# A state-space scan beside sliding-window attention: the last states of each group kept in another column order

## The chip, the cores and the metric

The kernel runs on one core of one Trainium2 chip. The metric is the device time of one execution in microseconds (us). PE is the matrix engine, DVE the vector engine, ACT the scalar engine, POOL and SP the two others; each executes its own stream of instructions in order, and semaphores connect them.

## The reference

Two independent parts, each on an input of 2048 positions by 448 channels, give the two halves of the output's last axis.

```python
# part A: a diagonal complex state-space model, 448 states
Lam_bar = exp(dt * Lam);  B_bar = ((Lam_bar - 1) / Lam)[:, None] * Bmat
h = 0
for t in range(2048):
    h = Lam_bar * h + B_bar @ x[t]
    y[t] = 2 * Re(Cmat @ h) + x[t] * Dskip
# part B: attention of 16 heads of 28, each query sees 8 keys, 2 positions apart
q, k, v = split(x @ wqkv)
attn = softmax(q . k[pos - 2*w] / sqrt(28), over w = 0..7, masked where pos - 2*w < 0)
out = (sum_w attn[w] * v[pos - 2*w]) @ wo
```

## The kernel before

**Part A** treats a complex state as two real rows: 64 states fill 128 partitions (64 real, 64 imaginary parts), so there are 7 blocks `m`. A multiplication by a power of Lam_bar is a 128x128 matrix, built for the powers 1, 2, 3, 4, 8, 12, 16, 32, ... up to 1024 (`mats`). Positions are cut into 512 groups of 4; `b` is the place in a group, and a column of 512 stands for the group. 512 groups are again 128 chunks `c` of 4 groups `a`, in column order `(c a)`.

- `level1` computes for each b and m the state within the group (`h[b]`, 512 columns): four matmuls with x, and one from the b before; ACT evicts it from PSUM (L450). `h[3]` is each group's own last state.
- `scan` gives the state at the end of each chunk of 16 positions. Its head (L460, L463) adds up the four groups of a chunk: the moving operands are the columns of one `a`, so every fourth column. Seven doubling steps (L470) then add the sum shifted by 1, 2, ... 64 chunks; the shifted operand lies in `pbuf`, with 64 zero columns ahead of it. After each step ACT copies the sum to `pbuf` (L474), and after the last to every fourth column of `G` (L476).
- `ends` gives the true state at the end of the three other groups of each chunk, from `h[3]` and from the carry, which is the chunk sum one chunk earlier, read from `G` at every fourth column. Six matmuls per m (L489, 1152 moving columns in all), and an eviction of 384 elements to every fourth column of `G` (L490). `G` starts with a zero column, so that `G[:, m, 0:512]` is the state ahead of each group.
- `correct` adds the carry to `h[0]` to `h[2]` (L496 to L498), and `y` forms the output of 128 groups for one b from seven blocks and the skip term (L509, L512, L515), 16 tiles in all.

The seven blocks are worked in two halves, m 0 to 3 and m 4 to 6 (`MH`). The program's order is level1, scan of half 0, level1, scan of half 1, ends 0, the corrections of half 0, ends 1, then y for b = 3, and per b the corrections of half 1 and y.

**Part B** projects q, k, v on PE, and forms the products with shifted keys and values on DVE (`qk`, L159 to L161; `pv`, L215 and L220), partly summed on PE (L164). `pv` goes through four groups of four positions; each group's result is transposed on PE (`pt_o`, L241, and for the last group L238, which also sums the last parts), evicted, multiplied by `wo` (L248) and stored. The products of a key group alternate between two `pr` buffers.

**Order.** The program emits part B's `pv` ahead of part A's level1; the framework decides at build time how each engine's stream interleaves them, after data dependences and the program's order as priority. PSUM tiles of the tag `mm` have three buffers, which level1, scan, ends, corrections and y share.

Of the kernel before, what the change touches and what calls it, by code (L numbers as in the profile page):

```python
# [12 lines left out]
f32 = mybir.dt.float32  # L13
bf16 = mybir.dt.bfloat16
# [4 lines left out]
NCH = 128  # L19
# [3 lines left out]
NF = 512  # L23
# [8 lines left out]
NM = 7  # L32
PL = 64
NST = 7
PAD = 64
MH = ((0, 4), (4, 7))
# [217 lines left out]
class PartA:  # L254
# [170 lines left out]
    def alloc_h(self):  # L425
        pool = self.pool
        self.h = [pool.tile([NCH, NM, 4 * NCH], bf16, name="h0", tag="xT1"),
                  pool.tile([NCH, NM, 4 * NCH], bf16, name="h1", tag="xT0"), pool.tile([NCH, NM, 4 * NCH], bf16, name="h2", tag="q1"),
                  pool.tile([NCH, NM, 4 * NCH], bf16, name="h3")]
        self.pbuf = [[pool.tile([NCH, m1 - m0, PAD + NCH], bf16, name=f"pbuf{m0}{i}") for i in range(2)]  # L430
                     for m0, m1 in MH]
        for pb in self.pbuf:
            for t_ in pb:
                self.nc.gpsimd.memset(t_[:, :, 0:PAD], 0.0)
        self.G = pool.tile([NCH, NM, 1 + NF], bf16, name="G", tag="q0")
        self.nc.gpsimd.memset(self.G[:, :, 0:1], 0.0)

    def level1(self, mh):
        nc, cx = self.nc, self.cx
        for b in range(4):  # L440
            for m in range(*MH[mh]):
                ps = cx.ps([NCH, 4 * NCH], f32, "l1", "mm")
                for k in range(KT):
                    nc.tensor.matmul(ps[:], lhsT=self.Bcat[:, k, m, :],  # L444
                                     rhs=self.xT[:, b, k, :],
                                     start=(k == 0), stop=(b == 0 and k == KT - 1))
                if b:
                    nc.tensor.matmul(ps[:], lhsT=self.mats[1][:, m, :], rhs=self.h[b - 1][:, m, :],  # L448
                                     start=False, stop=True)
                nc.scalar.copy(self.h[b][:, m, :], ps[:])  # L450

    def scan(self, mh):
        nc, cx = self.nc, self.cx
        M, v = self.mats, self.h[3]
        m0, m1 = MH[mh]
        pb = self.pbuf[mh]
        ps = cx.ps([NCH, m1 - m0, NCH], f32, "l2", "mm")
        for m in range(m0, m1):
            vm = v[:, m, :].rearrange("p (c a) -> p a c", a=4)
            nc.tensor.matmul(ps[:, m - m0, :], lhsT=cx.ident[:], rhs=vm[:, 3], start=(m == m0), stop=False,  # L460
                             skip_group_check=True)
            for i, p_ in enumerate((4, 8, 12)):
                nc.tensor.matmul(ps[:, m - m0, :], lhsT=M[p_][:, m, :], rhs=vm[:, 2 - i], start=False,  # L463
                                 stop=(i == 2), skip_group_check=True)
        nc.scalar.copy(pb[0][:, :, PAD:], ps[:])
        for s_ in range(NST):
            shf = 1 << s_
            src, dst = pb[s_ % 2], pb[(s_ + 1) % 2]
            for m in range(m0, m1):
                nc.tensor.matmul(ps[:, m - m0, :], lhsT=M[T << s_][:, m, :],  # L470
                                 rhs=src[:, m - m0, PAD - shf:PAD - shf + NCH], start=False, stop=True,
                                 skip_group_check=True)
            if s_ < NST - 1:
                nc.scalar.copy(dst[:, :, PAD:], ps[:])  # L474
            else:
                nc.scalar.copy(self.G[:, m0:m1, 1:].rearrange("p m (c a) -> p m c a", a=4)[:, :, :, 3], ps[:])  # L476

    def ends(self, mh):
        nc, cx = self.nc, self.cx
        M, v = self.mats, self.h[3]  # L480
        for m in range(*MH[mh]):
            vm = v[:, m, :].rearrange("p (c a) -> p a c", a=4)
            hp = self.G[:, m, 0:NF].rearrange("p (c a) -> p a c", a=4)[:, 0]
            ps = cx.ps([NCH, 3, NCH], f32, "gt", "mm")
            mm = [(cx.ident[:], vm[:, 0:3], 0, 3), (M[4][:, m, :], vm[:, 0:2], 1, 3), (M[8][:, m, :], vm[:, 0], 2, 3),
                  (M[4][:, m, :], hp, 0, 1), (M[8][:, m, :], hp, 1, 2), (M[12][:, m, :], hp, 2, 3)]
            for i, (l_, r_, c0, c1) in enumerate(mm):
                o_ = ps[:, c0:c1] if c1 - c0 > 1 else ps[:, c0]
                nc.tensor.matmul(o_, lhsT=l_, rhs=r_, start=(i == 0), stop=(i == 5), skip_group_check=True)  # L489
            nc.scalar.copy(self.G[:, m, 1:].rearrange("p (c a) -> p a c", a=4)[:, 0:3], ps[:])  # L490

    def correct(self, b, mh):
        nc, cx = self.nc, self.cx
# [131 lines left out]
```

## Time and profile before

| | |
|---|---|
| median of three runs | 171.19 us (170.5 to 171.29) |
| the profiled execution: time, span | 171.67 us, 169.9 us |
| granted PE clock | 0.997 |
| PE busy | 158.5 us (93%) |
| DVE busy | 146.0 us (86%) |
| ACT busy | 108.6 us (64%) |
| POOL busy | 3.6 us (2%) |
| DMA | 14.22 MB, mean 84 GB/s |

The span runs from the first to the last instruction; the time holds what lies around it as well. Busy shares are means over stages with different limits. In the groups, a number behind a line is the duration of one instruction, in ns; for a matmul that is its latency, and matmuls that follow each other overlap. Part A's level1 lies between 58 and 101 us, scans and ends between 81 and 120 us, and the y tiles from 121 us to the end.

### The profile page before, as it was taken

How to read it: one execution, taken by the hardware profiler on the slowest of the kernel's cores; microseconds unless marked ns; L12 is line 12 of the kernel's file. 1: busy time of each engine (PE TensorE's matmuls, PEld its weight loads, DVE VectorE, ACT ScalarE, POOL GpSimd, SP SyncE). 2: the span in 40 equal slices, each digit the busy share in tenths (PEclk: the TensorE clock that was granted, in tenths of full speed). 3: DMA queues.
4: the chain of work that ended last, by engine and by line, in shares of the span. 5: the costliest groups of instructions: out<-in, count | busy, mean ns of one | idle time of the engine just before them, and what ended most of it. 6: DMA issues, size and time to landing. Idle time of an engine off the chain costs nothing.

```text
span 169.9 us, 2983 instructions
## 1 busy us (share of the span) xinstructions
PE 158.5 (93%) x1152; PEld 92.1 (54%) x1162; DVE 146.0 (86%) x186; ACT 108.6 (64%) x206; POOL 3.6 (2%) x30
## 2 busy tenths in 40 slices
PE   7786999989999999999999999889999999999992
PEld 4453565555646564545664566436555655557750
DVE  1279999999999999999979999999999999990330
ACT  3194376647995788645568467999845765475241
POOL 8000000000000000000000000000000000000000
PEclk9999999999999999999999999999999999999998
DMA  5999756279945150000000000000122131212131
GB/s 167 298 287 196 117 105 161 85 207 203 165 88 152 62 161 4 0 0 0 0 4 0 0 0 4 0 0 0 54 86 82 46 120 58 81 54 100 41 106 54
DMA packets 23829, 14.22 MB, mean 84 GB/s; under 512 B 15855, under 2 KB 22923, under 8 KB 23815
## 3 DMA queue, kind: packets, MB, share of 16 engines
q1 hardware_dynamic: 23744, 14.03, 31.8%
q8 instruction: 9, 0.15, 0.4%
q14 instruction: 5, 0.04, 0.1%
q10 hardware_dynamic: 71, 0.01, 0.0%
HBM read 5.05 MB, written 3.67 MB: 51 GB/s over the span
## 4 chain that ended last, share of the span: by engine, by line
PE 63%; ACT 16%; DVE 13%; DMA 3%; issue 2%; ACTq 1%
PE l L444 12%; PE y_ps L512 12%; PE qkv_ps L141 8%; PE wo_ps L248 8%; DVE mat L395 4%; PE lg L164 4%; ACT Bcat L82 3%; PE l L448 3%; DMA drow<-in_A_Dskip_dram 3%; PE gt L489 2%; DVE pr L159 2%; ACT pbuf L474 2%; PE co L496 2%; PE pt_o L238 2%; DVE q L90 2%
## 5 line engine op out<-in xcount | busy, mean ns | idle before, releaser
L141 PE MATMUL qkv_ps<-wqkv_nat,xbT 112*128 112x448 bf16 x192 | 40.1, 352 | 1.9 <-DVE xbT L88 1.2
L215 DVE TENSOR_TENSOR pvb<-attn,vd 128x1792 bf16<-128x1792 bf16 (+1 forms) x33 | 34.0, 1050 | 0.0
L159 DVE TENSOR_TENSOR pr<-q,kd 128x3584 bf16<-128x3584 bf16 x16 | 31.7, 2018 | 1.2 <-PE lg L164 1.1
L444 PE MATMUL l<-xaT,Bcat 128*128 128x512 bf16 x106 | 29.1, 379 | 0.3
L141 PEld LDWEIGHTS <-xbT 112*128 112x128 bf16 x192 | 17.8, 97 | 16.9 <-DVE xbT L88 1.5
L220 DVE TENSOR_TENSOR pvb<-pvb 128x1792 bf16<-128x1792 bf16 x25 | 26.9, 1075 | 0.0
L450 ACT CAST h<-l 128x512 bf16<-128x512 f32 x28 | 16.3, 595 | 7.4 <-PE l L448 6.6
L512 PE MATMUL y_ps<-Ccat,h 128*128 128x448 bf16 x84 | 18.8, 352 | 0.0
L160 DVE TENSOR_TENSOR pr<-pr 128x1792 bf16<-128x1792 bf16 x16 | 16.8, 1083 | 0.0
L515 ACT CAST ya<-y_ps 128x448 bf16<-128x448 f32 x16 | 8.5, 534 | 12.4 <-PE y_ps L512 9.6
L444 PEld LDWEIGHTS <-Bcat 128*128 128x128 bf16 x112 | 10.6, 98 | 10.2 <-issue 0.2
L395 DVE TENSOR_TENSOR mat<-Dm,Scat 128x896 bf16<-128x896 f32 x13 | 14.1, 1082 | 0.0
L248 PE MATMUL wo_ps<-wo_p,oT 112*128 112x448 bf16 x64 | 13.5, 354 | 0.4
L498 ACT CAST h<-co 128x512 bf16<-128x512 f32 x21 | 11.3, 623 | 0.0
L82 ACT CAST yb<-wo_ps 128x448 bf16<-128x448 f32 x14 | 7.6, 541 | 4.9 <-PE wo_ps L248 4.7
L82 ACT CAST vd<-qkv_ps 128x448 bf16<-128x448 f32 x16 | 8.3, 534 | 3.3 <-PE qkv_ps L141 3.0
L82 ACT COPY xbT<-pt_x 112x512 bf16<-112x512 bf16 x12 | 7.0, 582 | 5.0 <-PE pt_x L134 5.0
L82 ACT CAST kd<-qkv_ps 128x448 bf16<-128x448 f32 x12 | 6.4, 532 | 5.6 <-PE qkv_ps L141 5.6
L512 PEld LDWEIGHTS <-h 128*128 128x128 bf16 x84 | 7.2, 98 | 4.8
L248 PEld LDWEIGHTS <-oT 112*128 112x128 bf16 x64 | 5.6, 98 | 7.4 <-ACT oT L82 3.0
L164 PE MATMUL lg<-pr,ident 128*128 128x128 bf16 x112 | 8.9, 219 | 0.4 <-DVE pr L161 0.4
L161 DVE TENSOR_TENSOR pr<-pr 128x896 bf16<-128x896 bf16 x16 | 9.2, 613 | 0.0
(131 smaller groups left out, 219.2 us busy)
## 6 DMA issues: line engine op xcount, KB each, us to landing
out_dram<-yb SPq DMA_DIRECT2D x16, 112.0 KB, 1.7
out_dram<-ya SPq DMA_DIRECT2D x16, 112.0 KB, 1.7
xb_sb<-in_B_x_dram SPq DMA_DIRECT2D x3, 448.0 KB
wqkv_nat<-in_B_wqkv_dram SPq DMA_DIRECT2D x3, 392.0 KB, 6.8
kd<-kd SPq DMA_DIRECT2D x1, 784.0 KB, 5.4
vd<-vd SPq DMA_DIRECT2D x1, 784.0 KB
kd<-kd SPq DMA_DIRECT2D x1, 588.0 KB, 4.2
vd<-vd SPq DMA_DIRECT2D x1, 588.0 KB
```

Of the source, the lines that this page charges most:

```text
L82: nc.scalar.copy(out, in_)
L141: nc.tensor.matmul(ps[:], lhsT=self.xT[j // 4][:, k, j % 4, :], rhs=self.wn[:, k, which, :], start=(k == 0), stop=(k == KT - 1))
L159: V.tensor_tensor(pr[:].rearrange("p d j h -> p j d h"), self.q[hf][:], self.kd[:, off:off + HJ], op=ALU.mult)
L160: V.tensor_tensor(pr[:, 0:14], pr[:, 0:14], pr[:, 14:28], op=ALU.add)
L164: nc.tensor.matmul(lgs[w // 4][:, w % 4, :], lhsT=cx.ident[:], rhs=pr[:, d].rearrange("p j h -> p (j h)"), start=(d == 0 and w % 4 == 0), ...
L215: V.tensor_tensor(t_[:, c0:c1], at[:, w, jl0 + c0:jl0 + c1, :].unsqueeze(2).to_broadcast([NCH, c1 - c0, DH, H]), self.vd[:, off + c0:off + ...
L220: V.tensor_tensor(acc[:, 0:n], acc[:, 0:n], t_[:, 0:n], op=ALU.add)
L248: nc.tensor.matmul(ps[:], lhsT=oT[:, kt, :], rhs=self.wo_p[:, kt, :], start=(kt == 0), stop=(kt == KT - 1))
L395: eng.tensor_tensor(t_[:], self.Dm[:].unsqueeze(1).unsqueeze(1).to_broadcast([NCH, NM, 2, PL]), scal.unsqueeze(3).to_broadcast([NCH, NM, 2 ...
L444: nc.tensor.matmul(ps[:], lhsT=self.Bcat[:, k, m, :], rhs=self.xT[:, b, k, :], start=(k == 0), stop=(b == 0 and k == KT - 1))
L450: nc.scalar.copy(self.h[b][:, m, :], ps[:])
L512: nc.tensor.matmul(ps[:], lhsT=self.state(m, r, b), rhs=self.C[:, m, :], start=False, stop=(m == NM - 1), skip_group_check=True)
```

## The change

The 512 columns of `h[3]` are stored as `(a c)` instead of `(c a)`: all chunks of the first group of a chunk, then those of the second, and so on. The order is made when ACT evicts `h[3]` (PSUM is then read with a step of four columns). The scan's head and the ends then take contiguous moving operands. The scan's last step is evicted to `pbuf` as the others are, and `ends` reads the carry from there, one column back. A seventh matmul per m copies the chunk sums into the ends' PSUM tile, and one eviction of 512 elements brings the tile back to `(c a)` in `G`: PSUM is read with a step of 128 columns, and `G` is written contiguously from its second column on. `G` is one column wider per m.

```diff
-        self.G = pool.tile([NCH, NM, 1 + NF], bf16, name="G", tag="q0")
+        self.G = pool.tile([NCH, NM, 2 + NF], bf16, name="G", tag="q0")
 ...
     def level1(self, mh):
-                nc.scalar.copy(self.h[b][:, m, :], ps[:])
+                if b < 3:
+                    nc.scalar.copy(self.h[b][:, m, :], ps[:])
+                else:
+                    nc.scalar.copy(self.h[b][:, m, :].rearrange("p (a c) -> p a c", a=4),
+                                   ps[:].rearrange("p (c a) -> p a c", a=4))
     def scan(self, mh):
-            vm = v[:, m, :].rearrange("p (c a) -> p a c", a=4)
+            vm = v[:, m, :].rearrange("p (a c) -> p a c", a=4)
 ...
-            if s_ < NST - 1:
-                nc.scalar.copy(dst[:, :, PAD:], ps[:])
-            else:
-                nc.scalar.copy(self.G[:, m0:m1, 1:].rearrange("p m (c a) -> p m c a", a=4)[:, :, :, 3], ps[:])
+            nc.scalar.copy(dst[:, :, PAD:], ps[:])
     def ends(self, mh):
+        hc = self.pbuf[mh][NST % 2]
         for m in range(*MH[mh]):
-            vm = v[:, m, :].rearrange("p (c a) -> p a c", a=4)
-            hp = self.G[:, m, 0:NF].rearrange("p (c a) -> p a c", a=4)[:, 0]
-            ps = cx.ps([NCH, 3, NCH], f32, "gt", "mm")
-            mm = [(cx.ident[:], vm[:, 0:3], 0, 3), (M[4][:, m, :], vm[:, 0:2], 1, 3), (M[8][:, m, :], vm[:, 0], 2, 3),
-                  (M[4][:, m, :], hp, 0, 1), (M[8][:, m, :], hp, 1, 2), (M[12][:, m, :], hp, 2, 3)]
+            vm = v[:, m, :]
+            hp = hc[:, m - MH[mh][0], PAD - 1:PAD - 1 + NCH]
+            ps = cx.ps([NCH, NF], f32, "gt", "mm")
+            mm = [(cx.ident[:], vm[:, 0:3 * NCH], 0, 3), (M[4][:, m, :], vm[:, 0:2 * NCH], 1, 3),
+                  (M[8][:, m, :], vm[:, 0:NCH], 2, 3), (M[4][:, m, :], hp, 0, 1), (M[8][:, m, :], hp, 1, 2),
+                  (M[12][:, m, :], hp, 2, 3), (cx.ident[:], hc[:, m - MH[mh][0], PAD:PAD + NCH], 3, 4)]
 ...
-            nc.scalar.copy(self.G[:, m, 1:].rearrange("p (c a) -> p a c", a=4)[:, 0:3], ps[:])
+            nc.scalar.copy(self.G[:, m, 1:1 + NF].rearrange("p (c a) -> p c a", a=4),
+                           ps[:].rearrange("p (a c) -> p c a", a=4))
```

More of the change, by code (lines that the diff above doesn't have):

```diff
@@ L480, in ends @@
         M, v = self.mats, self.h[3]
+        hc = self.pbuf[mh][NST % 2]
         for m in range(*MH[mh]):
-            vm = v[:, m, :].rearrange("p (c a) -> p a c", a=4)
-            hp = self.G[:, m, 0:NF].rearrange("p (c a) -> p a c", a=4)[:, 0]
-            ps = cx.ps([NCH, 3, NCH], f32, "gt", "mm")
-            mm = [(cx.ident[:], vm[:, 0:3], 0, 3), (M[4][:, m, :], vm[:, 0:2], 1, 3), (M[8][:, m, :], vm[:, 0], 2, 3),
-                  (M[4][:, m, :], hp, 0, 1), (M[8][:, m, :], hp, 1, 2), (M[12][:, m, :], hp, 2, 3)]
+            vm = v[:, m, :]
[4 more added lines that the diff above has]
+                  (M[12][:, m, :], hp, 2, 3), (cx.ident[:], hc[:, m - MH[mh][0], PAD:PAD + NCH], 3, 4)]
             for i, (l_, r_, c0, c1) in enumerate(mm):
-                o_ = ps[:, c0:c1] if c1 - c0 > 1 else ps[:, c0]
-                nc.tensor.matmul(o_, lhsT=l_, rhs=r_, start=(i == 0), stop=(i == 5), skip_group_check=True)
-            nc.scalar.copy(self.G[:, m, 1:].rearrange("p (c a) -> p a c", a=4)[:, 0:3], ps[:])
+                nc.tensor.matmul(ps[:, c0 * NCH:c1 * NCH], lhsT=l_, rhs=r_, start=(i == 0), stop=(i == 6),
+                                 skip_group_check=True)
+            nc.scalar.copy(self.G[:, m, 1:1 + NF].rearrange("p (c a) -> p c a", a=4),
+                           ps[:].rearrange("p (a c) -> p c a", a=4))
     def correct(self, b, mh):
```

## The prediction

> **What bounds the kernel now.** I read the page first, then the vector engine's waits, the chain of waits, the table of stretches, and the groups by shape. The page's bars say that two engines take turns as the limit:
>
> ```profile
> PE   7786999989999999999999999889999999999992
> DVE  1279999999999999999979999999999999990330
> ACT  3194376647995788645568467999845765475241
> ```
>
> From about 30 us to 153 us VectorE (DVE) is full; TensorE (PE) is full from the start of part A to the end; ScalarE (ACT) is full for a few slices around 105 us. The table of stretches (columns: length, then busy time of PE, weight loads, DVE, ACT) puts numbers on the three phases that matter:
>
> ```profile
> 103.40:112.20 8.80, 7.78 (x51) 4.41 (x50) 8.80 (x11) 8.68 (x15) 0.00 (x0) 1.00 0.01 2
> 127.10:142.10 15.00, 14.78 (x105) 8.37 (x105) 15.00 (x16) 9.53 (x19) 0.00 (x0) 1.00 0.23 78
> 153.30:169.90 16.60, 13.46 (x127) 8.66 (x125) 2.63 (x4) 5.78 (x11) 0.00 (x0) 0.97 0.21 70
> ```
>
> In the first ACT has no free moment, while PE idles 1.0 us. Later PE and DVE are both full. After DVE's last product, at 153.3, PE still has work to the end: not because DVE was late but because PE is behind it. The chain of waits shows that (start, length, what):
>
> ```profile
> 115.53 2.13 PE gt L489 x12
> 117.66 0.45 PE pt_o L241 x8
> ...
> 155.86 1.79 PE pt_o L238 x32
> ```
>
> The four groups of part B's accumulator leave DVE at 112.1, 127.1, 142.1 and 153.3 (starts and lengths in DVE's timeline); PE takes up their first transposes at 117.5, 132.3, 146.6 and 155.7 (its timeline). So PE runs 5.4, 5.2, 4.4 and 2.4 us behind. **PE's order from 115 us on is the path, and whatever makes PE arrive earlier shortens the kernel until it meets DVE.**
>
> The vector engine's own waits hold one line of interest:
>
> ```profile
> DVE pr L159 <- PE lg L164: 1.1, 1, 1.1
> ```
>
> At 86.96 DVE waits for PE, which has just come through the first scan's head.
>
> **The strided operands, priced.** The groups by shape:
>
> ```profile
> L470 PE MATMUL l<-pbuf,mat 128*128 128x128 bf16 x49 | 5.1, 220 | 0.2
> L463 PE MATMUL l<-h,mat 128*128 128x128 bf16 x21 | 3.4, 295 | 0.0
> L490 ACT CAST G<-gt 128x384 bf16<-128x384 f32 x7 | 7.3, 1040 | 0.9 <-PE gt L489 0.9
> L476 ACT CAST G<-l 128x512 bf16<-128x512 f32 x1 | 1.3, 1314 | 0.0
> L474 ACT CAST pbuf<-l 128x512 bf16<-128x512 f32 x6 | 3.5, 588 | 1.5 <-PE l L470 1.5
> ```
>
> L463 and L470 are the same matmul but for the moving operand's step (4 elements against 1): 295 against 220 ns. Those are latencies; the pitch counts. In the chain three L463 take 0.35 us, 116 ns each; eight contiguous transposes (L241) take 0.45, 56 ns each. So a step of four doubles the streaming time. L476 and L474 are the same eviction but for the written step: 1314 against 588 ns.
>
> **The change, part by part.**
>
> *Scan heads* (L460, L463): 28 matmuls go from 116 to 56 ns, 1.7 us: 0.97 in scan 0, 0.72 in scan 1.
>
> *Group ends* (L489): per m now 1152 columns in 1.01 us (115.43 to 116.44 in PE's timeline). After: 384 and 256 columns at the contiguous rate (0.16 + 0.11), and five 128-column matmuls, one of them the added copy of the carry (5 x 0.056): 0.55. Seven m save 3.2 us. The moving carry starts at an odd element; the first scan step (L470, shift 1) does that now, and L470's rows run 216 to 240 ns, so I charge nothing. PE in all: 4.9 us.
>
> *Ends' eviction* (L490): 7 x 1.04 us becomes 512 elements written contiguously, read from PSUM with a step of 128 f32. The nearest strided PSUM read is kd from qkv_ps (step 28 f32): 532 ns for 448 elements, as much as ya's contiguous 532. So I take 0.59, L474's price. Above: the write now starts at an odd element for every m, which no row shows; the dearest row is L476's 1.31. Below: contiguous L474 is the cheapest row of its size, so nothing less.
>
> *Scan's last eviction* (L476): 1.31 and 1.02 become L474's 0.59 and 0.48. *h3's eviction* (L450 at b = 3, seven): output contiguous, PSUM read at a step of 4: the same kd row says no extra; above, +0.73 each (1.31 less 0.59). G's one extra column only moves addresses.
>
> [...] L463's 116 ns pitch stands against 56 contiguous. [...]
>
> **Along the path**, engine orders held as they are:
> - 80.8 to 82.9: scan 0's head is 0.97 us shorter, but its last m needs the h3 evicted at 81.58, so 0.8 counts. PE is full behind it, so lg (L164, now 86.41) comes 0.8 earlier; its data was ready at 85.3. DVE's wait of 1.1 shrinks to 0.3 and **all of DVE's later work moves 0.8 earlier**.
> - Scan 1's head: 0.72. Sum 1.5.
> - 102.2 to 108.0, ends 0 and scan 1 interleaved: ACT's pair of evictions (G and pbuf) has a pitch of 1.31 to 1.36 us now (104.23, 105.54, 106.90). After, 0.38 (the pitch of an L474) + 0.49 (that of L498, 512 contiguous) = 0.87; PE's part, 0.55 + 3 x 0.056, fits below, and so does the step's own chain. Walked through, the first correction (L498, 108.04) comes 1.7 sooner relative to the head. Sum 3.2.
> - Then pbuf and h alternate at ACT's unchanged pace; L476's pitch goes from 0.76 to 0.38. Sum 3.6. Eight L498 at 0.51 are unchanged.
> - Ends 1, 115.4 to 119.2: three m on PE, 3 x 0.46 = 1.4, and its evictions no longer hold back oT. I count 1.3, for a wait on oT of 0.1. Sum 4.9.
>
> What caps it is DVE. The third transposes would come at 146.6 - 4.9 = 141.7; their data at 142.1 - 0.8 = 141.3. For the last, the parts are ready at 151.15, 152.15 and 152.72 (L215's cuts), and 24 of its 32 matmuls (1.3 us) go ahead of the one that needs the latest: PE may start at 151.4 without a stall, 150.6 after the 0.8. It would arrive at 155.7 - 4.9 = 150.8. So 4.9 just fits; without the 0.8 only 4.3 does. With margins of 0.2 to 0.4 I take **4.7 us**. Behind the last transposes nothing changes (14.0 us).
>
> The profiled execution took 171.67 us for its span of 169.9; it becomes 167.0. The median of the runs shown, 171.19, lies 0.5 lower, so I forecast **166.5**. Own range 165.5 to 168.0: all 4.9 and some luck with waits at one end, one more wait of over a microsecond at the other.
>
> **Rivals.**
> 1. *The gain stops at DVE* (0.14). The 0.8 is lost again in PE's waits around 87 us, and a new order of PE makes the last transposes wait for DVE's last instruction. Then PE gets only the lag of 2.4: 168.8. For: margins are tenths. Against: 24 of the 32 matmuls need older parts.
> 2. *The PSUM read costs what the strided write cost* (0.06). G's evictions then cost 1.31 instead of 1.04 and h3's 1.31 instead of 0.59. ACT's pair pitch is 1.6 against 1.3: +1.0 over four; h3 eats both scan heads' gain but 0.2; L476 and PE's ends 1 give back 0.4 and 1.0. About nothing is left, 0.3 us: 170.9. Against: kd's row. [...]
> 3. *The pitch was not the step's* (0.03): matmuls keep 116 ns, and the added copy costs that too. PE's 1.0 to 1.1 per m plus 0.2 to 0.35 for L470 then replaces ACT as pace at about 1.3; L476's 0.4 remains: 170.8.
> 4. *Slower* (0.10): PE's order is not the program's (transposes of part B stand between part A's matmuls), it is made anew at build, and PE executes in it. If the last transposes are placed ahead of more y tiles, PE waits for DVE and has these y tiles behind it. The end is 150.6 + 14.0 + 1.52 per y tile (four L509 and seven L512: 0.20 + 1.32). It passes today's 169.9 from 3.5 tiles on; at five it is 172.2, or 173.5 by the median. Against: PE's work only shrinks or, by element counts, grows by seven small matmuls, 0.4 us; that is a quarter of a tile.
>
> **The numbers.** Forecast 0.67, rivals 0.14, 0.06, 0.03, 0.10. A measurement here tells about 0.5% (0.9 us) from nothing. Faster: forecast and rival 1, 0.81. Same: rivals 2 and 3, 0.09. Slower: 0.10. The range 165.4 to 170.0 holds the forecast and rival 1, and a G eviction between the two bounds; 0.19 is left out.
>
> **What would show it.** Right: L460, L463 and L489 pitches near 56 ns per 128 columns; L490 (its new line) near 590 ns; DVE's wait on lg under 0.4; ACT's pbuf pitch near 0.9 around 102 us; first transposes of part B about 5 us earlier, within 1 us of DVE's hand-over; 14.0 us from the last transposes to the end. Wrong: an h3 or G eviction over 0.8 us, PE idle before pt_o L238 by over 1 us, or y tiles moved behind it.

## Result and profile after

The changed kernel takes 166.57 us (median of four, 165.99 to 166.86) against 171.12: a ratio of 0.974 (95% interval 0.970 to 0.977), 4.5 us less. The forecast was 166.5. The profiled execution took 166.39 us, its span 164.6. One profiled execution of a later experiment (a_yfirst) took 199.5 us at a granted PE clock of 0.76; it is a slow run, and no comparison uses it.

The groups by shape of the changed kernel (line, engine, operands, shapes, count; busy us, mean ns; idle time before) show what became of the strided instructions:

```profile
L467 PE MATMUL l<-h,mat 128*128 128x128 bf16 x21 | 1.9, 219 | 0.0
L491 PE MATMUL gt<-h,ident 128*128 128x384 bf16 x7 | 2.3, 325 | 0.0
L491 PE MATMUL gt<-pbuf,mat 128*128 128x128 bf16 x21 | 2.3, 220 | 0.0
L493 ACT CAST G<-gt 128x512 bf16<-128x512 f32 x7 | 4.3, 619 | 0.1
L477 ACT CAST pbuf<-l 128x384 bf16<-128x384 f32 x7 | 3.4, 484 | 0.0
L453 ACT CAST h<-l 128x512 bf16<-128x512 f32 x7 | 4.1, 588 | 2.3 <-PE l L448 2.3
```

L467 (L463 before) is down from 295 to 219 ns, L491 with the carry (L489) from 295 to 220. Those are latencies; the pitch stands in PE's timeline (start, length, what), where one m of the scan's head is one matmul with the identity and three with powers. Before, then after:

```profile
80.80 0.28 PE L460 MATMUL l<-h,ident 128*128 128x128 bf16 x1
...
81.24 0.30 PE L460 MATMUL l<-h,ident 128*128 128x128 bf16 x1
...
79.72 0.22 PE L464 MATMUL l<-h,ident 128*128 128x128 bf16 x1
...
79.94 0.22 PE L464 MATMUL l<-h,ident 128*128 128x128 bf16 x1
```

Four matmuls take 0.22 us now, 56 ns each, against 0.44 to 0.47. One m of the ends takes 0.55 us (110.47 to 111.02 in PE's timeline), against 1.01. G's eviction L493, now of 512 elements instead of 384, takes 0.62 us instead of 1.04. The h3 eviction L453, which now reads PSUM at a step of four, takes 588 ns, against 592 for the plain ones of its size (L451). So PE's moving operand paid for the step of 8 bytes, 116 ns per 128 columns against 56; ACT reads PSUM here at steps of 16, 112 and 512 bytes with no price that shows: L453 588 ns against L451's 592, kd 532 against the plain ya's 534, L493 619 against the plain L502's 615, means of the changed kernel's profile.

The vector engine's wait behind scan 0's head (lg is the partly summed product of part B that PE forms there):

```profile
DVE pr L159 <- PE lg L164: 0.3, 1, 0.3
```

It was 1.1; all of DVE's later work is 0.8 us earlier, counted from the head.

**A start that moves.** The spans differ by 5.3 us, but 1.1 of that is not the change: the first matmul of scan 0's head starts at 80.80 us in the profile of before and at 79.72 after, and in the other profiles of this study anywhere from 79.6 to 80.6. Of what the change edits, only evictions of h3 lie ahead of it, and they take as long as before. The chain of waits shows where the difference comes from: the first transfer that PE waits for, that of Dskip, took 1.1 us longer in the profile of before (before, then after; start, length, what):

```profile
2.38 4.48 DMA drow<-in_A_Dskip_dram
...
2.38 3.38 DMA drow<-in_A_Dskip_dram
```

From the matmul that takes it in (pt_d, at 7.00 and 5.90) to scan 0's head it is 73.80 and 73.81 us, and 73.8 to 74.0 in the ten other profiles. I therefore count from that head's first matmul to the end. This length repeats: 84.89, 84.88 and 84.89 us in two profiles of the changed kernel and one of an experiment that differs from it only in G's addresses, against 89.09 before. The kernel before has one profile alone, but two experiments that edit it only behind the first y tile (b_pe26, b_yorder) evict that tile at 43.67 us from the head, against its 43.69. **The change itself is worth 4.20 us.** The medians, 4.55 apart, hold the start's scatter too.

Counted from that matmul, with the prediction's running sum beside it:

| until | before | after | less | predicted |
|---|---|---|---|---|
| first pbuf eviction, scan 0 | 2.05 | 1.26 | 0.79 | 0.8 |
| first pbuf eviction, scan 1 | 21.64 | 20.07 | 1.57 | 1.5 |
| first correction evicted | 27.24 | 23.88 | 3.36 | 3.2 |
| start of the eight L498 (L502) | 31.45 | 27.67 | 3.78 | 3.6 |
| first y tile evicted | 43.69 | 38.58 | 5.12 | 4.9 |
| end | 89.09 | 84.89 | 4.20 | 4.7 |

Up to the first y tile the steps gave as much as forecast or a little more. Then 0.9 us was lost again, in a stage that the change does not touch. PE's timeline there shows where the four groups' transposes stand now (start, length, what). oT is a group as ACT evicts it between its transposes and the product with `wo`; ya and yb are output tiles, evicted ahead of their store. The last line is the last group's in the kernel before:

```profile
111.19 0.61 PE L241 MATMUL pt_o<-ident,pvb 128*112 128x128 bf16 x8
...
125.60 0.61 PE L241 MATMUL pt_o<-ident,pvb 128*112 128x128 bf16 x8
...
140.38 0.65 PE L241 MATMUL pt_o<-ident,pvb 128*112 128x128 bf16 x8
140.87 0.35 PE L516 MATMUL y_ps<-Ccat,h 128*128 128x448 bf16 x1
141.06 0.36 PE L513 MATMUL y_ps<-Dg,xaT 128*128 128x128 bf16 x4
141.49 1.69 PE L248 MATMUL wo_ps<-wo_p,oT 112*128 112x448 bf16 x8
...
149.40 2.19 PE L238 MATMUL pt_o<-ident,pvb 128*112 128x128 bf16 x32
...
155.70 1.95 PE L238 MATMUL pt_o<-ident,pvb 128*112 128x128 bf16 x32
```

DVE delivers the first three groups at 110.2, 125.2 and 140.25 (its timeline); PE takes them up 1.0, 0.4 and 0.1 us later, where it was over 4 us behind before. The last transposes begin 2.0 us ahead of DVE's last product (151.4) and take 2.19 us, not 1.95, because they meet parts that are not ready.

I went through the starts of PE's matmuls behind the first y tile and compared each distance with the streaming time of the matmul (a few distances twice as long, where a record is missing, left out). Before, PE waited 0.83 us in all, at three places, each for an oT eviction ahead of a wo. After, it waits for oT at five places, 1.28 us in all (0.30, 0.26, 0.23, 0.26, 0.23), and for DVE 0.63: 0.19 at the third group's transposes (0.15 ahead of them, 0.04 inside) and 0.44 at the last group's (0.20 ahead, 0.24 inside, where five of the 32 come 100 to 121 ns behind the one before instead of 56). Shorter gaps elsewhere make up a little of that: from the first y tile's eviction to the end it is 45.40 us before and 46.31 after, 0.91 more.

One of the experiments below, act_only, divides this loss. From the first y tile on its PE has the changed kernel's order of matmuls, waits 1.28 us for oT and never for DVE, and it takes 45.66 us for the same stretch. So the new order alone costs 0.26 us and the meeting with DVE 0.65.

Both come from the build's other order. Between the transposes and the first wo of the second and of the last group there now stand two y matmuls and one of 448 columns and some short ones, where three stood before, too little to cover the eviction. And y matmuls moved behind the transposes: of the 176, 120 instead of 124 now stand ahead of the third group's, and 142 instead of 148 ahead of the last group's. The six are two of 448 columns and four short ones, about 0.6 us by their pitch (0.19 and 0.05 us). So PE comes to the transposes sooner by more than it then waits there, and 15.2 us follow the start of the last ones instead of 14.2.

### The profile page after: what moved, and what is told of

Same layout as the page of the kernel before. It is cut to its first block, busy times and chain, and to the rows that moved or that the text cites. A ratio compares the mean times of both kernels' runs of the same rounds, so it can differ in the third digit from the quotient of the medians.

```text
span 164.6 us, 2998 instructions
## 1 busy us (share of the span) xinstructions
PE 154.3 (94%) x1159; PEld 89.2 (54%) x1169; DVE 146.0 (89%) x186; ACT 104.9 (64%) x206; POOL 3.6 (2%) x30
## 4 chain that ended last, share of the span: by engine, by line
PE 59%; ACT 20%; DVE 14%; issue 3%; DMA 2%; ACTq 1%
PE l L444 12%; PE y_ps L516 11%; PE wo_ps L248 8%; PE qkv_ps L141 8%; DVE mat L395 4%; PE lg L164 4%; ACT h L502 3%; ACT Bcat L82 3%; PE l L448 3%; ACT pbuf L477 3%; DVE pr L159 2%; PE pt_o L238 2%; ACT oT L82 2%; DMA drow<-in_A_Dskip_dram 2%; DVE q L90 2%
## 5 line engine op out<-in xcount | busy, mean ns | idle before, releaser
L451 ACT CAST h<-l 128x512 bf16<-128x512 f32 x21 | 12.2, 592 | 5.4 <-PE l L448 4.7
L502 ACT CAST h<-co 128x512 bf16<-128x512 f32 x21 | 11.1, 615 | 0.0
```

## Experiments

All times are medians, each compared with runs of the kernel before on the same chip; "from the head" is the length from the first matmul of scan 0's head to the end in the profile. The edits are shortened where three dots or a line of words stand.

**The head alone** (heads_only). Here the ends read h3 at the old step, and so take other columns than the reference does.

```diff
 level1: h3 evicted in (a c), as in the change
 scan:
-            vm = v[:, m, :].rearrange("p (c a) -> p a c", a=4)
+            vm = v[:, m, :].rearrange("p (a c) -> p a c", a=4)
```

> Only the scan's head gets contiguous columns (h3 stored as (a c)); the ends keep their step of four on h3, which there now picks other columns than the reference's, and both evictions to G stay strided. PE's order is that of the kernel before. If a step of four costs 60 ns per 128 columns and the heads lie on the path as the prediction walked it: L460 and L463 at a pitch of 56 ns, DVE's wait for lg down from 1.1 to 0.3 us, first pbuf eviction of scan 1 about 1.5 us earlier relative to the matmul ahead of scan 0's head, and 1.5 us off the time, 169.6 us. Rival (the pitch is not the step's): no change, 171.1. Rival (the saved time is idle elsewhere, ACT's chain or DVE takes it back): between 170.3 and 171.1.

169.46 us, ratio 0.991 (0.989 to 0.993); from the head 87.57 against 89.09, 1.52 less. The first pbuf evictions of scan 0 and 1 come at 1.26 and 20.12 from the head, as in the full change, and DVE's wait is the same 0.3. So the pitch is the step's, and the heads lie on the path: both rivals, no change and time taken back, fall.

**PE's part alone** (pe_only): as above, and the ends' operands from h3 contiguous too; evictions to G as before.

```diff
 ends:
-            vm = v[:, m, :].rearrange("p (c a) -> p a c", a=4)
+            vm = v[:, m, :].rearrange("p (a c) -> p a c", a=4)
```

> The matrix engine's part alone: h3 in (a c), contiguous operands in the head and for h3 in the ends; the carry is still read from G at a step of four, and both evictions to G stay strided, without the added copy. PE's order is that of the kernel before. PE saves 1.7 us in the heads and 7 x 0.36 = 2.5 in the ends. If ACT's evictions pace the ends of half 0 (pair pitch 1.31 us), their four m give nothing: 1.5 + 3 x 0.36 = 2.6 us off, 168.5. Rival (PE's own time is the path everywhere): 4.2 off, 166.9. In the trace, the first theory wants the pitch of the pbuf evictions around 103 us to stay at 1.3 us and PE's idle time there to grow.

168.20 us, ratio 0.984 (0.982 to 0.987); from the head 86.61, 2.48 less. Against the head alone, seven m of ends that are 0.36 shorter on PE gave 0.96, not 2.5: 0.43 up to the start of the eight corrections, from the four m of half 0, and 0.53 behind it, from the three of half 1. ACT's timeline in the ends of half 0 of this kernel says why (start, length, what, idle time before):

```profile
101.48 0.58 ACT L478 CAST pbuf<-l 128x384 bf16<-128x384 f32 x1
101.95 1.04 ACT L494 CAST G<-gt 128x384 bf16<-128x384 f32 x1
102.71 0.60 ACT L478 CAST pbuf<-l 128x384 bf16<-128x384 f32 x1
103.18 1.05 ACT L494 CAST G<-gt 128x384 bf16<-128x384 f32 x1
103.93 0.61 ACT L478 CAST pbuf<-l 128x384 bf16<-128x384 f32 x1
```

The pbuf evictions still come every 1.22 to 1.23 us (1.31 and 1.36 before), and ACT has no idle entry between them: it is the pace. PE's wait shows too: 0.5 us ahead of the ends' matmuls for an eviction to G, where the kernel before has none. In half 1 as well ACT has no idle entry around the ends (113.46 to 119.08 us). That the total, 2.48, is near the 2.6 expected is luck: half 0 was to give nothing and half 1 the full 1.1. In the changed kernel the same stretch reads

```profile
100.82 0.48 ACT L477 CAST pbuf<-l 128x384 bf16<-128x384 f32 x1
101.25 0.59 ACT L493 CAST G<-gt 128x512 bf16<-128x512 f32 x1
101.80 0.48 ACT L477 CAST pbuf<-l 128x384 bf16<-128x384 f32 x1
102.17 0.59 ACT L493 CAST G<-gt 128x512 bf16<-128x512 f32 x1
102.75 0.48 ACT L477 CAST pbuf<-l 128x384 bf16<-128x384 f32 x1
```

with 0.95 to 0.98 us from one to the next (0.87 was forecast).

**ACT's part alone** (act_only): the changed kernel with h3 left in (c a).

```diff
 level1: h3 evicted as before
 scan and ends:
-            vm = v[:, m, :]            # and (a c) in scan
+            vm = v[:, m, :].rearrange("p (c a) -> p a c", a=4)
```

> The scalar engine's part alone: h3 stays in (c a), so head and ends take h3 at a step of four; the carry goes to pbuf, the seventh matmul is there, and G is written by one contiguous eviction per m. PE's order is that of the changed kernel. PE per m of the ends is 0.92 us instead of 1.01. If ACT paced the ends of half 0, PE does so now, at 0.92 + 0.17 = 1.1 us per pair against 1.31: 0.9 us off over four, 0.4 from the scan's last eviction, 0.3 from ends 1: 1.6 us off, 169.5; up to 0.7 less where PE's other order waits more for oT: 170.2. Rival (evictions were hidden): 171.1 or above.

168.90 us, ratio 0.989 (0.987 to 0.991); from the head 87.30, 1.79 less (1.6 forecast). The pbuf pitch is 1.39 and 1.07, now with 0.20 of ACT's idle time waiting for PE:

```profile
102.77 0.48 ACT L473 CAST pbuf<-l 128x384 bf16<-128x384 f32 x1
103.37 0.59 ACT L489 CAST G<-gt 128x512 bf16<-128x512 f32 x1
104.16 0.48 ACT L473 CAST pbuf<-l 128x384 bf16<-128x384 f32 x1 [0.20 <-PE l L470]
```

PE's and ACT's parts, 2.48 and 1.79, add up to 4.27; together they give 4.20. That near equality hides two effects. Up to the first y tile the parts give 2.49 and 2.05, 4.54 in all, and the full change gives 5.12, because in the ends each engine holds back what the other has gained. Behind it pe_only loses nothing, act_only 0.26 and the full change 0.91.

**An even start for G** (g_even): two leading zero columns, so that G is written from an even element and the corrections read from the odd one.

```diff
-            nc.scalar.copy(self.G[:, m, 1:1 + NF].rearrange("p (c a) -> p c a", a=4),
+            nc.scalar.copy(self.G[:, m, 2:2 + NF].rearrange("p (c a) -> p c a", a=4),
 ...
-            nc.tensor.matmul(ps[:], lhsT=self.mats[b + 1][:, m, :], rhs=self.G[:, m, 0:NF], start=False, stop=True)
+            nc.tensor.matmul(ps[:], lhsT=self.mats[b + 1][:, m, :], rhs=self.G[:, m, 1:1 + NF], start=False, stop=True)
```

> The changed kernel with G's states from an even element on (two leading zero columns, the corrections' operand from the odd one). If an odd start of a contiguous bf16 write costs nothing, L493 stays at its mean of 0.62 us and the time at 166.6. If it costs, L493 falls below 0.59 and up to 0.3 us are gained; if odd starts cost on PE's moving operand instead, L501 rises above 0.38.

166.52 us, ratio 0.974 (0.972 to 0.976), from the head 84.89:

```profile
L493 ACT CAST G<-gt 128x512 bf16<-128x512 f32 x7 | 4.3, 614 | 0.1
L501 PE MATMUL co<-G,mat 128*128 128x512 bf16 x11 | 4.2, 377 | 0.0
```

614 against 619 ns for the write, and 377 ns for the moving operand at an odd element against 378 at an even one in the changed kernel. So an odd start shows no price here, neither in ACT's contiguous write nor in PE's moving operand; no row of the kernel before could tell that of the write.

**More work for PE, in both kernels** (b_pe26, a_pe26): is PE or DVE's hand-over the limit at the end? The corrections of half 1 for b = 0 and 1 get strided operands. The order of PE's matmuls stays each kernel's own.

```diff
 correct, for mh == 1 and b < 2:
+                pa = ps[:].rearrange("p (a c) -> p a c", a=4)
+                nc.tensor.matmul(pa, lhsT=cx.ident[:], rhs=self.h[b][:, m, :].rearrange("p (c a) -> p a c", a=4), ...)
+                nc.tensor.matmul(pa, lhsT=self.mats[b + 1][:, m, :],
+                                 rhs=self.G[:, m, 0:NF].rearrange("p (c a) -> p a c", a=4), ...)
+                nc.scalar.copy(self.h[b][:, m, :].rearrange("p (c a) -> p c a", a=4),
+                               ps[:].rearrange("p (a c) -> p c a", a=4))
```

> The kernel before, with 2.6 us more work on PE between the first and the third group of transposes: the corrections of half 1 for b = 0 and 1 take both moving operands at a step of four (12 matmuls of 512 columns, 215 ns more each) and the eviction puts the columns back. PE's order is that of the kernel before. PE lags DVE there by over 4 us, so all of it shows: 171.1 + 2.6 = 173.7. Rival (DVE's hand-over bounds the end): less, down to 171.1.

> The same 2.6 us of added PE work in the changed kernel, in its own order. If PE still is the path and DVE's hand-over costs it only the 0.1 to 0.3 us seen in the trace: 166.6 + 2.4 = 169.0. If the changed kernel is bound by DVE's hand-over at the last transposes (rival 1 of the prediction), part of it hides: about 1 us, 168.1, or less.

The kernel before goes to 173.17 (ratio 1.015, 1.012 to 1.018) and 91.89 from the head, 2.80 more: each of the twelve matmuls takes 0.24 us longer (forecast 0.215), which is again 60 ns per 128 columns. The changed kernel goes to 168.99 (ratio to before 0.989, 0.987 to 0.992) and 87.06 from the head, 2.17 more. PE is the path in both. In the changed one 0.63 us of the added work hides, as much as PE's waits for DVE came to there, and in this run's trace those waits are gone.

**The order at the end** (a_yfirst, a_yfirst2): two y tiles emitted at high priority.

```diff
         for a_ in range(4):
-            a.y(a_, b_)
+            if b_ == 2 and a_ < 2:
+                with tc.high_priority():
+                    a.y(a_, b_)
+            else:
+                a.y(a_, b_)
```

> The changed kernel with two y tiles of b = 2 emitted at high priority, so that 12 more y matmuls stand ahead of the last transposes (22 instead of 10; the kernel before has 16). If DVE's hand-over bounds the end (its part products ready at 150.8 in the profile), every y tile moved ahead of it shortens what follows: up to 12 x 0.19 = 2.3 us less, 164.3. If PE is the path, only its waits around the last transposes go: 0 to 0.4 us less, 166.2 to 166.6; the last transposes start 2.0 us later and there is no wait inside them, but their own tail (oT, wo, yb) has less to hide behind, so up to 0.3 more is possible.

> Two y tiles of b = 2 at high priority in the changed kernel (12 more y matmuls ahead of the last transposes), once more, for its trace, which the run before did not give in a usable form. PE-bound theory: the waits for DVE at the last transposes go (0.20 ahead of them and 0.06 inside): 84.6 from the head to the end, against 84.9. Bound by DVE's hand-over: up to 2.3 less, 82.6.

165.84 us (ratio 0.972, 0.969 to 0.975) and, again, 166.32 (0.974, 0.971 to 0.976). The changed kernel beside the second run:

> The changed kernel, unedited, beside the two below on one chip: 166.5 us, and 84.9 us in its trace from the first matmul of scan 0's head to the end, as in its first profile.

166.90 us, ratio 0.976 (0.974 to 0.978), 84.88 from the head. The edited kernel has 84.47, 0.41 less, about what PE waits for DVE at the last group in the changed kernel (0.44). The expectation's 2.3 priced all twelve moved y matmuls at 0.19 us; eight have 448 columns and four are short, and the last transposes start 1.58 us later from the head. That the gain is 0.41 and not 1.6 is the plainest sign that DVE does not bound the end. The last group meets nothing unready: its 32 matmuls start 55 or 56 ns apart (20 of them in this stretch's view):

```profile
148.47 2.62 PE L516 MATMUL y_ps<-Ccat,h 128*128 128x448 bf16 x13
150.93 1.28 PE L238 MATMUL pt_o<-ident,pvb 128*112 128x128 bf16 x20
```

It is the fastest version here in both runs' medians; the intervals overlap the changed kernel's, so it is the length from the head that shows the gain.

**More of the same** (a_yorder, b_yorder): six y tiles, (b, r) = (0, 0), (0, 1), (1, 2), (1, 3), (2, 0), (2, 1), at high priority, in the changed kernel and in the one before.

> The changed kernel with six y tiles at high priority: 9, 2 and 12 y matmuls more ahead of the second, third and last group's transposes, and seven instead of four between the second group's first transposes and its wo. PE-bound theory with the waits as counted in the trace: the waits on DVE at the third and last group go (0.14 + 0.20 + 0.06) and one wait for oT of 0.3 becomes filled: 0.6 to 0.7 less than the changed kernel, 165.9, and 84.2 to 84.3 from the head to the end. If the order is of no account: 166.5 and 84.9.

> The same six priorities in the kernel before (5 and 6 y matmuls more ahead of the second and last group's transposes; seven y matmuls instead of three ahead of one wo). PE lags DVE by 2.4 us and more there, so nothing waits for DVE and only fillers ahead of wo change: within 0.3 us of 171.0, and 88.8 to 89.2 from the head to the end. If it gains as much as the changed kernel does, the waits on DVE are not what the order removes.

Both expectations failed. The changed kernel goes to 167.66 (0.981, 0.979 to 0.983), 85.75 from the head: 0.86 more instead of 0.6 less. The kernel before goes to 172.90 (1.011, 1.009 to 1.014), 90.96 from the head: 1.87 more. In a_yorder the waits for DVE did go (the third and the last group's transposes start 55 to 57 ns apart), but new waits came. PE's timeline there:

```profile
145.15 1.69 PE L248 MATMUL wo_ps<-wo_p,oT 112*128 112x448 bf16 x8
146.67 0.54 PE L516 MATMUL y_ps<-Ccat,h 128*128 128x448 bf16 x2
147.94 0.38 PE L500 MATMUL co<-h,ident 128*128 128x512 bf16 x1 [0.72 <-ACT ya L519]
```

The corrections for b = 2 leave PE idle for 0.72 us until a y eviction, and their third pair for 0.24 us until an eviction of the corrections' own (L502); by the distances between starts the two are 0.88 and 0.40 us. ACT's timeline shows two ya evictions queued behind the oT and yb evictions of the third group:

```profile
146.92 0.53 ACT L82 CAST yb<-wo_ps 128x448 bf16<-128x448 f32 x1 [0.22 <-PE wo_ps L248]
147.35 0.97 ACT L519 CAST ya<-y_ps 128x448 bf16<-128x448 f32 x2
148.56 1.07 ACT L502 CAST h<-co 128x512 bf16<-128x512 f32 x2 [0.24 <-PE co L501]
```

The y tiles hold PSUM buffers of the tag that the corrections need. Whether the buffer alone is the cause was not tried with a fourth one. In b_yorder the same two distances ahead of the corrections appear, again 0.88 and 0.40 us longer than the matmuls take, and that kernel has no waits for DVE to lose.

## Why the prediction was right

**Price of the step.** 60 ns per 128 columns on PE, 0.4 us and more per eviction to G: L467 and L491 came to the 56 ns and the 0.55 us per m that were forecast, L493 to 0.62 us for 0.59.

**Scan heads.** 0.8 and 0.72 forecast, running sum 1.5; 0.79 and 1.57 measured, and heads_only gives 1.52 to the end. The detail that scan 0's last m must wait for its h3 eviction held, and DVE's wait shrank to the 0.3 named.

**Ends of half 0, paced by ACT.** 1.7 forecast, 1.79 measured (3.36 less 1.57). The pair pitch is 0.95 to 0.98, not 0.87, but the first eviction to G comes 0.48 sooner, behind a shorter first m on PE. pe_only shows the pace: PE's shorter matmuls alone give 0.43 there.

**Scan's last eviction and ends 1.** 0.4 and 1.3 forecast; 0.42 and 1.33 measured.

**Odd start, strided PSUM read.** Both taken as free, and neither shows a price: the write to G takes 614 ns from an even element (g_even) and 619 from an odd one, and the reads at a step 588 (L453) and 619 (L493) against 592 and 615 for plain ones of their size. Rival 2 is out. Rival 3 (the pitch is not the step's) falls with heads_only.

**The cap.** The prediction held the engines' orders as they were, allowed 0.2 us of its sum of 4.9 for the meeting with DVE, and said that behind the last transposes nothing changes (14.0 us in its chain, 14.2 from their first matmul). That step failed. The build put the last transposes ahead of six more y matmuls, 15.2 us follow their start, and 0.92 of the 5.12 gained up to the first y tile was lost again. act_only divides that loss: about 0.26 from waits for oT in the new order, 0.65 from waits for DVE. So rival 1's mechanism, a new order of PE that makes transposes wait for DVE, happened and cost 0.65 us, not the 2.3 that rival 1 would have cost; DVE's own 0.8 was not lost (its last product comes 0.79 earlier from the head). Rival 4's mechanism, y matmuls behind the last transposes, happened as well: six of them, about 0.6 us, not the 3.5 tiles that would have made the kernel slower.

**Near by luck in part.** The mechanism held, but 166.5 against 166.57 is closer than the terms. The sum up to the first y tile was 0.2 too low and the allowance for what follows 0.7 too low: 4.20 where 4.7 was forecast. The medians fell by 4.55, since they hold the start's scatter of a microsecond as well.

## What to carry to other kernels

Price a strided operand by the pitch of consecutive instructions, find the same instruction with a contiguous operand in the same trace, and put the step where the trace shows no price for it: here, into ACT's read of PSUM (588 ns at a step of four, 592 without). Where two engines alternate, as in the ends, shortening one of them can give less than its own saving (pe_only: 0.96 us of 2.5); the pair's pace must be walked through. When a gain brings one engine up to the hand-over of another, the order in which the build interleaves them becomes worth tenths of a microsecond, in either direction (0.41 less in a_yfirst2, 0.86 more in a_yorder), so compare the orders before trusting a sum that holds them fixed.

## What was not expected of the hardware

The stretch from scan 0's head to the end repeats to 0.01 us between two executions of the changed kernel (84.89 and 84.88), while its start scatters by 1.2 us (79.6 to 80.8 us in twelve profiles). Nearly all of that scatter arises in the first 7 us, at the landing of one transfer (Dskip's, 4.48 us before and 3.38 after): from the matmul that takes it in to the scan's head it is 73.80 to 73.89 us in eleven of the twelve profiles and 74.03 in the other. For changes under one per cent such a length, read from the profile, tells more than the medians.
